# A Fourier filter and a gated two-layer network on one core: the small operations of a normalization moved to GpSimd, chunks of y taken one step later, a third PSUM tile

## The chip, the cores and the metric

The kernel runs on one core of one Trainium2 chip. The metric is the device time of one launch in microseconds, the median of several runs; the times below are for the kernel before the change.

## What is computed

The input x has 4 batches of 3072 tokens with 256 channels. Three blocks follow one another:

```python
X = np.fft.rfft(x, axis=1)                      # filter: along the 3072 tokens
Yr = Xr @ w_r - Xi @ w_i + b_r ; Yi = Xr @ w_i + Xi @ w_r + b_i
Y  = soft_threshold(Yr, 0.01) + 1j * soft_threshold(Yi, 0.01)
y  = np.fft.irfft(Y, n=3072, axis=1)

h = relu(y @ w_in); u, v = h[..., :512], h[..., 512:]
v_n = (v - mean(v)) / sqrt(var(v) + 1e-6)       # per token, over 512 channels
v_s = einsum('ts,bsd->btd', w_spatial, v_n) + b_spatial
x2  = (u * v_s) @ w_out

r = relu(x2 @ w2_in); out = (s * r * r + b) @ w2_out
```

## The kernel before

Three stages follow each other. `attention` does the filter, then the product that gives v, and the normalization of v; `mixing` does the 3072 x 3072 product `w_spatial @ v_n` by a scheme of block sums; `output` does the rest. The change lies in `attention` alone. All products run in two or three passes over a high and a low part of each fp32 operand, so each operand is split: a ScalarE cast gives the high part and a subtraction gives the low one.

The filter is a two-step transform. `s1` is the first step of the forward transform, `g_stage` the second, `mix` the complex product, `g2_stage` the first step of the inverse, and `s3` the last one: 128 calls, 32 for a batch. Between the steps the data goes through DRAM. Four calls of `s3` make one chunk of y (384 tokens), and `v_product` turns a chunk into three tiles of v (128 tokens by 512 channels); three tiles form one normalization group, so there are 32 chunks, 96 products and 32 groups.

The order of the work is written out by hand. Each call issues its matmuls at once and hands its evacuation, as a list of stages, to `Chains`: `ch.step()`, which nearly every call makes once, issues the next stage of every live chain, oldest first; `ch.add` issues the first stage of a new one. `wait` (line 165) is a stage that does nothing. So a chain of n stages is spread over n steps, and every engine then runs its own queue in the order of issue.

For a group, the chain of its third product holds these stages, one per step after the product: `wait`, `stats` (two VectorE operations), `spread` (line 588, variance plus epsilon, 128 x 3), a ScalarE square root (line 612), `rstd` (lines 591 to 596: a reciprocal, two Newton rounds of three operations, one product with the mean; all on VectorE, all 128 x 3, each reading what the one before it wrote), `normal(0)` and `normal(1)`, `normal(2)`, and `store`, three DMAs issued by GpSimd. `normal` runs on ScalarE (line 600) or VectorE (line 602). GpSimd also makes the low parts of x, t and v (line 295).

The chain of the fourth `s3` of a chunk has the stages: ScalarE copy `y_t` of half of the PSUM tile (line 481), VectorE sum `y_sb` (line 463), `store` on the SP queue, `high` (line 472), `low` (line 476), `ready`, which lets `v_product` take the chunk.

The main loop runs over k from 0 to 49 and mixes calls of all stages. After it, `tail[0]` is set and the last loop does what is left of `s3` and `v_product`, about 40 calls of `s3`; each of its turns prefetches one tile for `mixing`, calls `s3_more`, then `v_product` if a chunk is ready, else only `ch.step()`. `s3_more` makes a `v_hi` cast (ScalarE) and a `v_lo` subtraction (GpSimd) in every second turn.

PSUM has four pools in this stage: `pg` (one tile of two banks, used by `g_stage`), `pm`, `pa` and `py` (two tiles of one bank each). The tiles of `s3` come from `py`, so the matmuls of one call wait until the sum `y_sb` of the call two before has read its tile. In the last loop `pg` lies idle.

Of the kernel before, what the change touches and what calls it, by code (L numbers as in the profile page):

```python
# [9 lines left out]
F32 = mybir.dt.float32  # L10
# [5 lines left out]
ALU = mybir.AluOpType  # L16
# [6 lines left out]
N1 = 96  # L23
# [8 lines left out]
EPS = 1e-6  # L32


def f(ap):
    return ap.bitcast(F32)
# [191 lines left out]
def attention(tc, nc, x, w_r, w_i, b_r, b_i, c_f, c_b, c_g, c_v, c_s, zd, vd, yd, vn, chunks, cd, follow, nb=NB):  # L228
# [10 lines left out]
    pg = banks("a_pg", 1, space=PSUM)  # L239
    pm = banks("a_pm", 2, space=PSUM)  # L240
    pa = banks("a_pa", 2, space=PSUM)
    py = banks("a_py", 2, space=PSUM)
    ch = Chains()
# [199 lines left out]
        ch.add([evac])  # L443

    ys = {}

    def s3(j):
        b, n = divmod(j, N2)
        c, o = divmod(n, 4)
        vs.make(j // 2 + 1)  # L450
        hi, lo = vs.t[j // 2]
        ps = py.tile([128, 2, 2, N1], F32, tag="py", name="ps_y")
        for h in range(2):
            for m, t in enumerate((hi, lo)):
                nc.tensor.matmul(ps[:, h].rearrange("p k a -> p (k a)"), t[:, o % 2, h * 128:(h + 1) * 128], cb,
                                 start=m == 0, stop=m == 1)
        if o == 0:
            ys[0] = s3p.tile([128, 2, 4, N1], F32, tag="y_sb", name="y_sb")
        y = ys[0]
        tmp = s3p.tile([128, 2, N1], F32, tag="y_t", name="y_t")  # L460

        def e1():
            nc.vector.tensor_add(y[:, :, o, :], ps[:, :, 0, :], tmp)

        def store():
            (nc.sync if steady[0] else nc.gpsimd).dma_start(
                out=yd[b].rearrange("h p s -> p h s")[:, :, c * 4 * N1:(c + 1) * 4 * N1],
                in_=y.rearrange("p h n a -> p h (n a)"))

        def high():  # L470
            y_hl[8 * b + c] = t = vpool.tile([128, 2, 2, 4 * N1], F32R, tag="y_hl", name="y_hl")
            nc.scalar.copy(t[:, 0], y.rearrange("p h n a -> p h (n a)"))

        def low():
            t = y_hl[8 * b + c]
            nc.vector.tensor_sub(t[:, 1], y.rearrange("p h n a -> p h (n a)"), f(t)[:, 0])

        def ready():
            chunks_ready[0] += 1
        ch.step()  # L480
        ch.add([lambda: nc.scalar.copy(tmp, ps[:, :, 1, :]), e1] + ([store, high, low, ready] if o == 3 else []))

    y_hl = {}
    chunks_ready = [0]
# [1 line left out]
    root = s3c.tile([128, 1], F32, name="root")  # L486
# [73 lines left out]
    def v_product():  # L560

        n = v_done[0]
        v_done[0] += 1
        y = y_hl[n // 3]
        o = (n % 3) * 128
        pool, tag = (pm, "pm") if tail[0] and n % 2 else (pa, "pa")
        ps = pool.tile([128, 512], F32, tag=tag, name="ps_vp")
        c = 0
        for k in range(2):
            for a, w in PASSES:  # L570
                nc.tensor.matmul(ps, y[:, a, k, o:o + 128], win[k][:, w, :], start=c == 0, stop=c == 5)  # L571
                c += 1
        vr = vpool.tile([128, 512], F32, tag="vr", name="vr", bufs=VR)
        bn = vpool.tile([128, 6], F32, tag="bn", name="bn")
        j = n % 3
        if j == 0:
            grp[0] = (vpool.tile([128, 3, 2], F32, tag="mv", name="mv"),
                      vpool.tile([128, 5, 3], F32, tag="rs", name="rs"), [])
        mv, t, vrs = grp[0]
        vrs.append(vr)  # L580
        va, r, z, root, nmr = (t[:, m, :] for m in range(5))

        def stats():
            nc.vector.bn_stats(bn, vr)
            nc.vector.bn_aggr(mv[:, j, :], bn)

        def spread():
            nc.vector.tensor_scalar_add(va, mv[:, :, 1], EPS)

        def rstd():  # L590
            nc.vector.reciprocal(r, root)
            for _ in range(2):
                nc.vector.tensor_mul(z, r, r)
                nc.vector.scalar_tensor_tensor(out=z, in0=z, scalar=-0.5, in1=va, op0=ALU.mult, op1=ALU.mult)
                nc.vector.scalar_tensor_tensor(out=r, in0=z, scalar=1.5, in1=r, op0=ALU.add, op1=ALU.mult)
            nc.vector.scalar_tensor_tensor(out=nmr, in0=mv[:, :, 0], scalar=-1.0, in1=r, op0=ALU.mult, op1=ALU.mult)

        def normal(m):
            if m == 0 or m == 2 and n // 3 % 2 == 0:
                nc.scalar.activation(vrs[m], vrs[m], AF.Identity, bias=nmr[:, m:m + 1], scale=r[:, m:m + 1])  # L600
            else:
                nc.vector.tensor_scalar(vrs[m], vrs[m], r[:, m:m + 1], nmr[:, m:m + 1], op0=ALU.mult, op1=ALU.add)

        def store():
            b, i = divmod(n - 2, 24)
            for m in range(3):
                nc.gpsimd.dma_start(out=vn[b][i + m], in_=vrs[m])
        ch.step()
        nc.scalar.activation(vr, ps, AF.Relu)
        rest = [wait, stats]  # L610
        if j == 2:
            rest += [spread, lambda: nc.scalar.sqrt(root, va), rstd, lambda: (normal(0), normal(1)),
                     lambda: normal(2), store]
        ch.add(rest)

    tail = [False]

    def v_some():
        if v_done[0] < 3 * chunks_ready[0]:
            v_product()  # L620

    for k in range(total + 2):
# [6 lines left out]
        def s3_some(n):  # L629
            nonlocal s3_done  # L630
            for _ in range(n):
                if s3_done < s3_goal:
                    s3(s3_done)
                    s3_done += 1
        if 4 <= k < 16:
            j, h = divmod((k - 4) // 3, 2)
# [34 lines left out]
    def s3_more():  # L671
        nonlocal s3_done
        if s3_done < 32 * nb:
            vs.load(s3_done // 2 + 4)
            s3(s3_done)
            s3_done += 1
            vs.make(s3_done // 2 + 2)
# [3 lines left out]
    while v_done[0] < NV:  # L681
        stage.prefetch()
        s3_more()
        if v_done[0] < 3 * chunks_ready[0]:
            v_product()
        else:
            ch.step()
        if s3_done == 32 * nb:
            ch.step()
        if v_done[0] in (NV - 3, NV - 1):  # L690
            stage.split_first()
# [470 lines left out]
def network(ctx, tc, ins, out):  # L1162
# [25 lines left out]
    with tc.manual_schedule():  # L1188
        attention(tc, nc, ins['x'], ins['w_r'], ins['w_i'], ins['b_r'], ins['b_i'],
                  ins['c_f'], ins['c_b'], ins['c_g'], ins['c_v'], ins['c_s'], zd, vd, yd, vn, chunks, cd,  # L1190
                  lambda: mixing(tc, nc, ins['moe_w_spatial'], vn, md, sd, convert_half)).run()
        output(tc, nc, yd, md, chunks, cd, ins['moe_b_spatial'], ins['moe2_s'], ins['moe2_b'], out)
# [25 lines left out]
```

## Time and profile before the change

| what | value |
|---|---|
| median of 3 runs | 3199.53 us (3198.64 to 3200.73) |
| profiled execution, own time | 3198.13 us |
| its span | 3196.0 us |
| PE busy | 3091.2 us (97%) |
| DVE busy | 2307.5 us (72%) |
| ACT busy | 1427.7 us (45%) |
| POOL busy | 391.2 us (12%) |
| `attention`, to the first matmul burst of `mixing` | about 0 to 568 us |

Times are from the span's start. PE is TensorE, DVE is VectorE, ACT is ScalarE, POOL is GpSimd. Busy shares are means over three stages with different limits; the change can be judged only inside the first 570 us.

### The profile page before, as it was taken

What the parts mean: (1) busy time and instruction counts of PE and PEld (TensorE: products, weight loads), DVE (VectorE), ACT (ScalarE), POOL (GpSimd) and SP (SyncE); (2) the same over time, 40 slices, a digit from 0 to 9 for tenths busy, and PEclk for the clock granted to TensorE, in tenths of its full rate; (3) what the DMA queues carried; (4) which work ended last, traced back from release to release, by engine and by line L of the source; (5) the groups of instructions that cost most, each with busy time, mean ns of one, the idle gap of its engine ahead of it and who ended that gap; (6) DMA issues with size and microseconds to landing.
All of it is one profiled execution on the core that took longest, in us unless ns stands there. A gap on an engine that the chain in (4) does not pass through costs nothing.

```text
span 3196.0 us, 46503 instructions
## 1 busy us (share of the span) xinstructions
PE 3091.2 (97%) x17960; PEld 3016.2 (94%) x17960; DVE 2307.5 (72%) x3495; ACT 1427.7 (45%) x2243; POOL 391.2 (12%) x497
## 2 busy tenths in 40 slices
PE   7989998999999999999999999999999999999999
PEld 4988986999999999999999989999999999999999
DVE  5877988887878888888878755656566656656564
ACT  4776766433334333433434334444444444444443
POOL 2665544022000210000000100000000000000000
PEclk9999999999999999999999999999999999999999
DMA  7987759487456956466471621111111111110210
GB/s 233 288 264 236 232 173 332 158 310 298 159 198 195 356 216 230 147 214 257 152 244 38 238 90 54 48 50 65 55 65 55 65 55 65 55 62 30 71 45 15
DMA packets 230517, 488.30 MB, mean 153 GB/s; under 512 B 22356, under 2 KB 116376, under 8 KB 230296
## 3 DMA queue, kind: packets, MB, share of 16 engines
q1 hardware_dynamic: 197112, 353.44, 33.4%
q0 software_dynamic: 33184, 131.90, 11.2%
q8 instruction: 140, 2.29, 0.3%
q14 instruction: 81, 0.66, 0.1%
HBM read 322.72 MB, written 162.53 MB: 152 GB/s over the span
## 4 chain that ended last, share of the span: by engine, by line
PE 76%; DVE 13%; DMA 5%; ACT 3%; issue 2%; POOL 0%; SPq 0%; ACTq 0%; DVEq 0%; POOLq 0%
PE acc L849 27%; PE ps_h L1059 17%; PE oacc L1080 17%; PE ps_o L1040 4%; PE ps_u L1022 4%; PE ps_m L407 3%; PE ps_vp L571 2%; DMA st_a<-in_moe_w_spatial_dram 1%; DVE kept L866 1%; DVE a_hl L830 1%; DVE b_hl L830 1%; DMA st_b<-t 1%; PE ps_z L333 1%; DMA st_b<-vn 1%; PE ps_g L360 1%
## 5 line engine op out<-in xcount | busy, mean ns | idle before, releaser
L849 PE MATMUL acc<-a_hl,b_hl 128*128 128x384 f32 x7056 | 1240.7, 337 | 30.4 <-DVE kept L866 11.5
L849 PEld LDWEIGHTS acc<-a_hl,b_hl 128*128 128x128 f32 x7056 | 1234.3, 189 | 36.8 <-ACT kept L870 11.9
L1059 PE MATMUL ps_h<-x_hl,w 128*128 128x384 f32 x3072 | 580.8, 337 | 1.5 <-ACT x_hl L1043 0.9
L1080 PE MATMUL oacc<-q_hl,w 128*128 128x384 f32 x3072 | 575.5, 337 | 0.5 <-DVE q_hl L1066 0.5
L1059 PEld LDWEIGHTS ps_h<-x_hl,w 128*128 128x128 f32 x3072 | 543.4, 188 | 2.1 <-ACT x_hl L1043 1.3
L1080 PEld LDWEIGHTS oacc<-q_hl,w 128*128 128x128 f32 x3072 | 537.1, 188 | 0.9 <-DVE q_hl L1066 0.8
L826 ACT CAST a_hl<-a 128x768 fp32r<-128x768 f32 x253 | 211.7, 837 | 522.6 <-PE acc L849 440.8
L1066 DVE TENSOR_TENSOR q_hl<-r,q_hl 128x768 fp32r<-128x768 f32 x256 | 245.4, 959 | 230.7 <-ACT q_hl L1065 230.7
L1064 DVE TENSOR_TENSOR r<-r 128x768 f32<-128x768 f32 x256 | 244.8, 956 | 204.6 <-ACT r L1063 204.6
L1065 ACT CAST q_hl<-r 128x768 fp32r<-128x768 f32 x256 | 213.6, 835 | 301.7 <-DVE r L1064 301.7
L1063 ACT ACTIVATE r<-ps_h 128x768 f32<-128x768 f32 x256 | 208.2, 813 | 310.9 <-PE ps_h L1059 307.4
L830 DVE TENSOR_TENSOR a_hl<-a,a_hl 128x768 fp32r<-128x768 f32 x253 | 241.2, 953 | 138.4 <-ACT a_hl L826 137.8
L830 DVE TENSOR_TENSOR b_hl<-b,b_hl 128x512 fp32r<-128x512 f32 x295 | 201.8, 684 | 0.0
L826 ACT CAST b_hl<-b 128x512 fp32r<-128x512 f32 x295 | 181.8, 616 | 0.0
L571 PE MATMUL ps_vp<-win,y_hl 128*128 128x512 f32 x576 | 155.7, 407 | 17.8 <-ACT v_sb L438 14.7
L867 POOL DMA_DIRECT2D md<-kept x112 | 60.5, 540 | 828.9 <-DVE kept L866 824.5
L1022 PE MATMUL ps_u<-y_hl,w 128*128 128x384 f32 x768 | 145.7, 340 | 1.8 <-DVE y_hl L1008 1.8
L1040 PE MATMUL ps_o<-g,w 128*128 128x384 f32 x768 | 139.3, 337 | 1.6 <-DVE g L1030 1.0
L571 PEld LDWEIGHTS ps_vp<-win,y_hl 128*128 128x128 f32 x576 | 103.2, 193 | 39.8 <-ACT v_sb L438 16.3
L1022 PEld LDWEIGHTS ps_u<-y_hl,w 128*128 128x128 f32 x768 | 135.5, 190 | 3.1 <-DVE y_hl L1008 2.1
L1040 PEld LDWEIGHTS ps_o<-g,w 128*128 128x128 f32 x768 | 133.5, 188 | 2.5 <-DVE g L1030 1.6
L866 DVE TENSOR_TENSOR kept<-acc,kept 128x768 f32<-128x768 f32 x112 | 102.8, 950 | 22.0 <-PE acc L849 21.0
(138 smaller groups left out, 3702.5 us busy)
## 6 DMA issues: line engine op xcount, KB each, us to landing
a<-in_moe_w_spatial_dram SPq DMA_DIRECT2D x144, 384.0 KB, 4.8
b<-vn SPq DMA_DIRECT2D x168, 256.0 KB, 4.9
md<-kept POOLq DMA_DIRECT2D x112, 384.0 KB, 5.2
m<-md SPq DMA_DIRECT2D x56, 768.0 KB, 6.4
st_a<-in_moe_w_spatial_dram SPq DMA_DIRECT2D x72, 384.0 KB, 5.4
vn<-vr POOLq DMA_DIRECT2D x96, 256.0 KB, 4.0
s<-a POOLq DMA_DIRECT2D x48, 384.0 KB, 5.8
x_f<-in_x_dram SPq DMA_DIRECT2D x32, 384.0 KB, 6.1
```

The lines of the kernel that those rows point to most:

```text
L571: nc.tensor.matmul(ps, y[:, a, k, o:o + 128], win[k][:, w, :], start=c == 0, stop=c == 5)
L826: nc.scalar.copy(s[:, 0, :], t)
L830: sub(s[:, 1, :], term.pop((kind, n)), f(s)[:, 0, :])
L849: nc.tensor.matmul(acc[d][:, h, 0:TH], b[:, m, d * 128:(d + 1) * 128], a[:, w, h * TH:(h + 1) * TH], start=fresh and i == 0 and c == 0, st ...
L1022: nc.tensor.matmul(ps[:, d, 0:TH], win[k][:, a, o:o + 128], y[:, w, k, :], start=c == 0, stop=c == 5)
L1040: nc.tensor.matmul(ps[:, h, 0:TH], wo[k // 2][:, a, o:o + 128], g[:, w, k, :], start=c == 0, stop=c == 11)
L1059: nc.tensor.matmul(ps[:, e, 0:TH], w[:, a, o:o + 128], x[:, i, j, :], start=c == 0, stop=c == 5)
L1063: nc.scalar.activation(r, ps[:, :, 0:TH], AF.Relu)
L1064: nc.vector.tensor_mul(r, r, r)
L1065: nc.scalar.copy(s[:, 0], r)
L1066: nc.vector.tensor_sub(s[:, 1], r, f(s)[:, 0])
L1080: nc.tensor.matmul(ps[:, h, 0:TH], w[:, a, o:o + 128], s[:, i, e, :], start=ff == 0 and c == 0, stop=ff == 2 * NP - 1 and c == 2)
```

## The change

- `spread` runs on GpSimd.
- In `rstd` only the reciprocal stays on VectorE. The seven VectorE operations behind it become ten GpSimd operations: each Newton round has four in place of three, and the product with the mean has two in place of one. All are 128 x 3 and each reads what the one before it wrote.
- A `wait` stage stands between `rstd` and the normals, which are issued one step later, and so are the three stores of a group.
- A `wait` stage stands between `low` and `ready` of a chunk.
- In the last loop every third call of `s3` takes its PSUM tile from `pg`.

```diff
     def s3(j):
-        ps = py.tile([128, 2, 2, N1], F32, tag="py", name="ps_y")
+        if tail[0] and j % 3 == 0:
+            ps = pg.tile([128, 4, 256], F32, tag="pg", name="ps_y")[:, 0:2, 0:2 * N1].rearrange(
+                "p h (k a) -> p h k a", k=2)
+        else:
+            ps = py.tile([128, 2, 2, N1], F32, tag="py", name="ps_y")
...
-        ch.add([lambda: nc.scalar.copy(tmp, ps[:, :, 1, :]), e1] + ([store, high, low, ready] if o == 3 else []))
+        ch.add([lambda: nc.scalar.copy(tmp, ps[:, :, 1, :]), e1] + ([store, high, low, wait, ready] if o == 3 else []))
...
         def spread():
-            nc.vector.tensor_scalar_add(va, mv[:, :, 1], EPS)
+            nc.gpsimd.tensor_scalar_add(va, mv[:, :, 1], EPS)
 
         def rstd():
             nc.vector.reciprocal(r, root)
+            g = nc.gpsimd
             for _ in range(2):
-                nc.vector.tensor_mul(z, r, r)
-                nc.vector.scalar_tensor_tensor(out=z, in0=z, scalar=-0.5, in1=va, op0=ALU.mult, op1=ALU.mult)
-                nc.vector.scalar_tensor_tensor(out=r, in0=z, scalar=1.5, in1=r, op0=ALU.add, op1=ALU.mult)
-            nc.vector.scalar_tensor_tensor(out=nmr, in0=mv[:, :, 0], scalar=-1.0, in1=r, op0=ALU.mult, op1=ALU.mult)
+                g.tensor_mul(z, r, r)
+                g.tensor_mul(z, z, va)
+                g.tensor_scalar(z, z, -0.5, 1.5, op0=ALU.mult, op1=ALU.add)
+                g.tensor_mul(r, z, r)
+            g.tensor_mul(nmr, mv[:, :, 0], r)
+            g.tensor_scalar_mul(nmr, nmr, -1.0)
...
-            rest += [spread, lambda: nc.scalar.sqrt(root, va), rstd, lambda: (normal(0), normal(1)),
+            rest += [spread, lambda: nc.scalar.sqrt(root, va), rstd, wait, lambda: (normal(0), normal(1)),
                      lambda: normal(2), store]
```

## Rows read from the trace of the kernel before

**Rows 1.** Busy time by stretch: main loop, last loop, its end; us and instruction counts.

```profile
core 0: us, PE busy (x) PEld busy (x) DVE busy (x) ACT busy (x) POOL busy (x), PEclk, DMA share, GB/s
182.00:470.00 288.00, 271.08 (x1854) 248.79 (x1852) 246.61 (x572) 197.53 (x432) 146.02 (x147) 0.98 0.67 219
476.00:556.00 80.00, 65.22 (x340) 50.18 (x338) 70.67 (x212) 53.52 (x122) 38.71 (x47) 1.00 0.94 329
556.00:576.00 20.00, 13.34 (x56) 11.76 (x56) 16.54 (x43) 11.77 (x20) 4.14 (x8) 0.83 0.35 128
```

**Rows 2.** Groups on DVE, 182 to 470 us: busy us, mean ns | idle before, releaser.

```profile
L594 DVE SCALAR_TENSOR_TENSOR rs<-rs 128x3 f32<-128x3 f32 x40 | 18.3, 459 | 1.4
L593 DVE TENSOR_TENSOR rs<-rs 128x3 f32<-128x3 f32 x40 | 11.0, 276 | 1.4
L595 DVE SCALAR_TENSOR_TENSOR rs<-rs 128x3 f32<-128x3 f32 x40 | 8.6, 214 | 1.4
L588 DVE TENSOR_SCALAR rs<-mv 128x3 f32<-128x3 f32 x20 | 7.6, 382 | 0.7 <-issue 0.2
L596 DVE SCALAR_TENSOR_TENSOR rs<-mv,rs 128x3 f32<-128x3 f32 x20 | 5.4, 269 | 0.7
```

**Rows 3.** Two groups on PE: the first of 182 to 470, the second of 476 to 556.

```profile
L571 PE MATMUL ps_vp<-win,y_hl 128*128 128x512 f32 x348 | 94.7, 408 | 13.6 <-ACT v_sb L438 11.9 <-ACT vr L609 0.8 <-DVE y_hl L476 0.8
...
L455 PE MATMUL ps_y<-cb,v_hi 96*128 96x192 f32 x78 | 21.1, 296 | 14.8 <-DVE y_sb L463 14.7
```

**Rows 4.** Timeline at 318 us: start, duration, engine, line, operation [idle before].

```profile
318.63 2.40 POOL L295 TENSOR_TENSOR t_l<-t_f,t_h 128x1024 fp32r<-128x1024 f32 x1 [5.23 <-ACT t_h L291]
318.67 2.38 DVE L594 SCALAR_TENSOR_TENSOR rs<-rs 128x3 f32<-128x3 f32 x1
```

**Rows 5.** Timeline at 465 to 471 us, one group of the main loop.

```profile
464.93 2.53 POOL L295 TENSOR_TENSOR v_lo<-v_f,v_hi 96x512 fp32r<-96x512 f32 x2 [4.47 <-ACT v_hi L291]
...
466.20 1.29 DVE L593 TENSOR_TENSOR rs<-rs 128x3 f32<-128x3 f32 x1
...
467.52 0.17 DVE L594 SCALAR_TENSOR_TENSOR rs<-rs 128x3 f32<-128x3 f32 x1
...
468.71 0.81 ACT L600 ACTIVATE vr<-vr,rs 128x512 f32<-128x512 f32 x1 [2.52 <-DVE rs L596]
...
470.56 2.03 PE L571 MATMUL ps_vp<-win,y_hl 128*128 128x512 f32 x4 [2.21 <-ACT v_sb L438]
```

**Rows 6.** The two groups on ACT that wait for the small operations, 476 to 556.

```profile
L600 ACT ACTIVATE vr<-vr,rs 128x512 f32<-128x512 f32 x15 | 12.2, 816 | 9.2 <-DVE rs L596 9.2
...
L612 ACT ACTIVATE rs<-rs 128x3 f32<-128x3 f32 x10 | 2.0, 204 | 16.7 <-DVE rs L588 16.7
```

**Rows 7.** Timeline of one group in the last loop, 494 to 499 us.

```profile
494.28 0.62 ACT L291 CAST v_hi<-v_f 96x512 fp32r<-96x512 f32 x1
...
495.29 1.29 POOL L295 TENSOR_TENSOR v_lo<-v_f,v_hi 96x512 fp32r<-96x512 f32 x1
...
495.62 1.01 DVE L588 TENSOR_SCALAR rs<-mv 128x3 f32<-128x3 f32 x1
...
496.66 0.20 ACT L612 ACTIVATE rs<-rs 128x3 f32<-128x3 f32 x1 [1.75 <-DVE rs L588]
...
496.77 0.30 ACT L481 COPY y_t<-ps_y 128x192 f32<-128x192 f32 x1
...
498.49 0.81 ACT L600 ACTIVATE vr<-vr,rs 128x512 f32<-128x512 f32 x1 [0.93 <-DVE rs L596]
```

**Rows 8.** Chain that ended last, in order of time: start, us, what; eight chunks apart.

```profile
485.33 0.86 DVE y_hl L476
...
550.46 0.87 DVE y_hl L476
```

**Rows 9.** Timeline of POOL at the span's start: a write without a read.

```profile
0.28 0.10 POOL L1199 MEMSET const-float32-1.0<- 128x1 f32 x1
```

**Rows 10.** Busy time by stretch, in `mixing`, columns as in the first group.

```profile
730.00:740.00 10.00, 10.00 (x59) 10.00 (x58) 5.28 (x8) 3.24 (x6) 2.16 (x4) 1.00 1.03 417
```

More of the change, by code (lines that the diff above doesn't have):

```diff
@@ L445, in attention @@
     ys = {}
+    tail = [False]
     def s3(j):
@@ L611, in v_product @@
         if j == 2:
-            rest += [spread, lambda: nc.scalar.sqrt(root, va), rstd, lambda: (normal(0), normal(1)),
+            rest += [spread, lambda: nc.scalar.sqrt(root, va), rstd, wait, lambda: (normal(0), normal(1)),
                      lambda: normal(2), store]
         ch.add(rest)
-    tail = [False]
     def v_some():
```

## Prediction, made before the changed kernel ran

> **What bounds the kernel now.** I read the busy time by stretch first, then the groups of instructions in two stretches, then timelines of single groups of the normalization, and last the chain that ended last. All of the change lies before 570 us, and there in two places with different limits.
>
> In the main loop, 182 to 470 us, PE is busy 271.1 of 288 us [rows 1]; at most 17 us are to be had there. DVE is at 246.6, ACT at 197.5, POOL at 146.0. The operations that the change takes off DVE make 18.3 + 11.0 + 8.6 + 7.6 + 5.4 = 50.9 us of its 246.6 [rows 2], for 20 groups. Yet PE hardly waits for DVE: 11.9 of its idle time is a product that waits for ScalarE's copy `v_sb` to free a PSUM tile, and 0.8 for a low part of y [rows 3]. Rows 5 show where such a wait comes from: GpSimd makes two low parts from 464.93 to 467.46; the small operation at 466.20, 0.17 us at its neighbour, takes 1.29 and ends when GpSimd does; ScalarE stands 2.52 us before the normal at 468.71; `v_sb` comes late and PE loses 2.21. Rows 4 show the same with a larger GpSimd subtraction: 2.38 beside 2.40. So in the main loop the cost is a stall of ScalarE, in order, behind the small operations.
>
> In the last loop, 476 to 556 us, no engine is full: PE 65.2 of 80, DVE 70.7, ACT 53.5, POOL 38.7 [rows 1]. Eight chunks take 550.46 - 485.33 = 65.1 us, so 8.14 us for each [rows 8]. ScalarE explains them: 53.5 us busy and 16.7 + 9.2 = 25.9 us of standing before the square root and the normals [rows 1, 6], 79.4 of 80. Per group that is 1.67 before the square root and 0.92 before the normals. A circle of dependences therefore sets the pace: normals, ScalarE's own queue, statistics, `spread`, square root, Newton rounds, next normals. PE's 14.7 us of waiting for `y_sb` [rows 3] follow from it.
>
> **The change part by part.** *Price of a small GpSimd operation.* No row shows one with inputs. A `v_lo` of 512 elements takes 1.29, a `t_l` of 1024 takes 2.40 [rows 7, 4]: 2.17 ns an element, and 2 x 1.29 - 2.40 = 0.18 us for none. To the next that depends on it there is a gap: on DVE 467.52 - 467.49 = 0.03 [rows 5]. With 0.03 to 0.10 I get 0.21 to 0.28 and take 0.25. Bounds: 0.10, the write without a read [rows 9]; 0.36, if the passage from one to the next costs as much as the operation. So 11 operations are 2.75 us of GpSimd per group (1.1 to 4.0).
>
> *`spread` and `rstd` in the last loop.* A chunk has eight steps, and the chunk's order of issue is: step 1 `v_hi` and `v_lo`, step 2 `spread`, step 3 the square root, step 4 `rstd`, step 5 (now 6) the normals, step 5 another `v_hi` and `v_lo`, and the stores at the end. Before, DVE's `spread` ran at 495.62 while GpSimd had the `v_lo` of 495.29, and took 1.01; it ended 0.05 after it [rows 7]. After, `spread` stands in GpSimd's queue right behind that same `v_lo`. It waits for it as before and then takes 0.25: from the end of the cast to the square root 1.29 + 0.25 + about 0.1 for gaps = 1.65, against 1.67 now. Nothing is won there. Before the normals, ten operations of 0.25 replace seven that start 0.20 apart (467.52 less 467.49 plus 0.17): 2.5 against 1.4, so +1.1. The added step lets ScalarE do a copy and a cast of 0.30 and 0.62 [rows 7] first; they overlap their neighbours by some 0.1 each, so -0.7. The stall becomes 0.92 + 0.4 = 1.3. Both together: 2.95 for 2.59, +0.36 per chunk, and with ten groups in the stretch **+4 us**. At 0.36 per operation it is 1.75 + 2.4 = 4.15, +15 us. At 0.10 it is 1.5 + 0 = 1.5, -11 us, but the DMA engines stop it earlier: they move 329 GB/s at a share of 0.94 here, 350 at a full share [rows 1], so the stretch's 26.3 MB need 75.2 us, -5. (With the 417 of [rows 10] it would be 63; that stretch only loads, so I keep -5.) Behind the waiting square root and normals on ScalarE stand `y_t`, `v_hi`, `y_hl` and the Relu that frees the product's PSUM tile; s3 and the products on PE wait for these. Behind a waiting operation on GpSimd stand `v_lo` and the stores of vn. `v_lo` is made two pairs ahead, more than three turns before its matmuls, so a delay of 2.75 us is hidden by some 6 us; without that lead it would be paid in each chunk.
>
> *The same in the main loop.* The groups come 14.4 us apart (288 / 20), so no circle sets the pace, only single stalls count. DVE is relieved of 50.9 / 20 = 2.5 us per group. The chain takes 2.5 in place of 1.4 plus what GpSimd's port took (43.3 - 140 x 0.17 = 19.5 us for 20 groups, 1.0), which now comes back as GpSimd's own queue; so +1.1, against a step of 0.7 to 1.0 that lies between. The stall of the normals stays about what it was. But what ScalarE does in that step is in part the evacuation that PE waited for: in rows 5 `v_sb` can come before the normal, not after. I give back a third of the 11.9 us: **-4**. Bounds: -12 (all of it) and +6, if `spread` behind a subtraction of 1.29 holds the square root by 0.3 more in each of 20 groups.
>
> *The stores of vn* come a step later: one microsecond of a buffer of nine tiles, three chunks long. Nothing. No DMA moves on the SP queue.
>
> *Chunks of y a step later.* In the last loop two steps make a turn and the chunk is looked for in the second one: `ready` moves from the fifth step to the sixth, both before the same look. Nothing. In the main loop a product can move by one slot; it can save the 0.8 us of [rows 3] and cost as much: 0, +-1.
>
> *The third PSUM tile.* It lets `s3` wait for the sum of three calls before and can remove the 14.7 us of [rows 3]. The pace is set elsewhere, so they become slack: 0. Were PE the limit, it would be worth up to 1.5 us per chunk; that is in the lower end of the range. `pg` is free by then.
>
> *The end of the stage*, 556 to 576: one group's `spread` no longer waits for splits on DVE, its chain is 1.1 longer: 0, +-1.
>
> **Sum.** +4 - 4 + 0 = 0 against the profiled 3198.13, whose median of runs is 1.4 higher: 3199.5, so **3200**.
>
> **A rule against the change.** Rows 4 and 5 show a DVE operation that ends with the GpSimd operation beside it. The Trainium skill, "SBUF — State Buffer", section "SBUF: two separate sides", says that the two share a port pair which the first holds alone for a whole instruction; by that rule, with which these rows agree, the stall does not vanish but passes to DVE's next operation with two inputs, such as `low`. The Trainium skill, "Perfetto Trace Analysis", section "Optimizing Scalar/DVE Operations", says that moving work between these two may not help for this reason. This is the third rival below.
>
> **The rivals.**
> 1. *Relief* (0.29). Small operations cost 0.10 to 0.15, and ScalarE's stalls shrink. For it: DVE's 50.9 + 20 us of work gone, PE free in the last loop by the third tile. Against it: 0.18 by the two subtractions, and the DMA share of 0.94. It gives -5 in the last loop and -8 in the main one: **3186**.
> 2. *GpSimd's queue becomes the limit* (0.26). Place: `spread` behind `v_lo`, and the chain of ten, both in ScalarE's way. From 0.30 per operation on it decides: there the last loop has 1.7 + 1.8 = 3.5 for 2.59, +9, and the main loop's -4 falls to about +2: **3211**. For it: the circle above has no slack. Against it: the step that hides 0.7.
> 3. *The stalls change their owner* (0.10). DVE's other operations wait for GpSimd instead, PE sees nothing in the main loop: 0, and +4 in the last: **3203.5**.
>
> **How the numbers follow.** The forecast, 3200, has 0.35. A measurement here tells about 0.2%, 6.4 us, from no change. Forecast and rival 3 lie within it (0.45); faster 0.29, slower 0.26. The forecast's own range is 3193 to 3207. To leave out no more than 2 in 10 it reaches to rival 1 and rival 2 with the bounds of the price: 3184 to 3214.
>
> **What would show it.** Small GpSimd operations start 0.21 to 0.28 apart; ScalarE's stalls in the last loop near 1.65 and 1.3 per group; chunks there 8.4 to 8.6 us apart; PE's waits for `y_sb` there near zero; in the main loop DVE near 196 us busy and PE's waits for `v_sb` near 8 us. It is wrong if the small operations lie outside 0.15 to 0.30, if the DMA engines carry far over 350 GB/s in the last loop, or if the time is won or lost behind 576 us.

## The result, and the profile after

The changed kernel takes **3227.05 us**, the median of 6 runs (3223.10 to 3231.71), beside 3200.34 us for the kernel before on the same chips (6 runs, 3198.64 to 3203.80). The ratio is 1.008 [1.007, 1.009]: 26.7 us slower. The prediction said 3200 and its range ended at 3214. The profiled execution took 3229.8 us, its span is 3226.5.

The loss lies ahead of the product of `mixing`, in two places. The last matmul of the main loop's inverse stage (`g2_stage`, L433) starts at 474.7 us before and at 489.6 after: +15. The last product of v ends at 561.9 before and at 588.5 after, so the last loop takes 98.9 us in place of 87.2: +11.7. Busy time by stretch, each kernel with its own ends of the two loops (columns as in [rows 1]). Before:

```profile
182.00:475.00 293.00, 275.52 (x1873) 252.65 (x1871) 249.60 (x579) 199.68 (x437) 147.66 (x149) 0.98 0.67 218
475.00:562.00 87.00, 70.77 (x364) 54.39 (x363) 75.97 (x224) 58.41 (x131) 39.64 (x48) 1.00 0.90 316
```

After:

```profile
182.00:490.00 308.00, 281.34 (x1869) 256.63 (x1868) 210.90 (x416) 199.57 (x435) 194.97 (x368) 0.96 0.64 205
490.00:589.00 99.00, 83.41 (x365) 66.04 (x365) 69.58 (x149) 59.81 (x132) 63.82 (x164) 0.84 0.86 284
```

The work did move: DVE 249.6 to 210.9 in the main loop, POOL 147.7 to 195.0. Yet TensorE needs longer for the same number of matmuls. In the main loop 9.2 of the 15 us are more idle time (26.7 for 17.5) and 5.8 are longer matmuls: the granted clock is 0.96 for 0.98. In the last loop its idle time is the same (15.6 for 16.2), and the matmuls take 12.6 us more at a granted clock of 0.84 for 1.00.

The waits say where the relief went. Main loop, ACT and then DVE of after (engine, line, what it waited for: us in total, times, longest):

```profile
ACT vr L608 <- POOL rs L604: 46.3, 20, 4.0
...
ACT yh L420 <- DVE mt L419: 15.2, 20, 2.2
ACT rs L620 <- POOL rs L593: 12.1, 13, 2.1
...
DVE vr L610 <- POOL rs L604: 52.4, 20, 5.1
```

The same of before, ACT:

```profile
ACT vr L600 <- DVE rs L596: 41.0, 20, 4.0
...
ACT yh L420 <- DVE mt L419: 3.6, 7, 0.9
ACT rs L612 <- DVE rs L588: 3.4, 4, 1.3
```

The change took 50.9 us of small operations off VectorE [rows 2], and VectorE now stands for 52.4 us before its own normal (L610) until GpSimd has finished them; before, this wait did not exist, since VectorE had made the numbers itself. ScalarE stands 25.6 us more in three places: 5.3 before the normals, 8.7 before the square root, 11.6 before `yh`, which waits for VectorE. Its waits for TensorE's products of v are 10.4 us shorter (17.5 for 27.9).

One group of the last loop, beside [rows 7] (start, duration, engine, line, operation, idle before):

```profile
521.79 1.28 POOL L295 TENSOR_TENSOR v_lo<-v_f,v_hi 96x512 fp32r<-96x512 f32 x1 [1.40 <-ACT v_hi L291]
...
523.16 0.23 POOL L593 TENSOR_SCALAR rs<-mv 128x3 f32<-128x3 f32 x1
...
523.42 0.20 ACT L620 ACTIVATE rs<-rs 128x3 f32<-128x3 f32 x1 [1.71 <-POOL rs L593]
...
523.66 0.18 DVE L596 RECIPROCAL rs<-rs 128x3 f32<-128x3 f32 x1 [1.11 <-ACT rs L620]
...
523.92 0.20 POOL L599 TENSOR_TENSOR rs<-rs 128x3 f32<-128x3 f32 x1 [0.53 <-DVE rs L596]
...
524.20 0.19 POOL L600 TENSOR_TENSOR rs<-rs 128x3 f32<-128x3 f32 x1
...
526.43 0.23 POOL L604 TENSOR_SCALAR rs<-rs 128x3 f32<-128x3 f32 x1
...
526.64 1.26 POOL L295 TENSOR_TENSOR v_lo<-v_f,v_hi 96x512 fp32r<-96x512 f32 x1
526.70 0.81 ACT L608 ACTIVATE vr<-vr,rs 128x512 f32<-128x512 f32 x1 [1.64 <-POOL rs L604]
526.70 1.48 DVE L610 TENSOR_SCALAR vr<-vr,rs 128x512 f32<-128x512 f32 x1 [1.41 <-POOL rs L604]
```

The small operations start 0.28 us apart (523.92 to 524.20; ten from 523.92 to 526.66). From the end of the reciprocal to the normals it is 526.70 - 523.84 = 2.86 us; before, from 496.89 + 0.19 = 497.08 (the reciprocal on the chain shown at the end of this section) to the normal at 498.49 in [rows 7], it was 1.41. Then `v_lo`, next in GpSimd's queue, starts together with VectorE's normal, which takes 1.48 where it took 0.54 before. VectorE's fifteen normals of the last loop take 16.6 us in place of 8.0.

The chain that ended last shows the pace of the last loop (start, us, what). After, two chunks between each of these, so 9.09 us for a chunk; before it was 8.14 [rows 8]:

```profile
537.81 0.74 ACT y_hl L477
...
555.98 0.74 ACT y_hl L477
...
574.16 0.74 ACT y_hl L477
```

Before, that chain ran almost wholly on one engine. Between 490 and 507 us all its pieces but one stretch on ScalarE (499.21 to 501.26) are VectorE's, one behind the other, with the small operations among them:

```profile
496.62 0.26 DVE y_sb L463
...
496.89 0.19 DVE rs L591
...
498.29 0.04 DVE rs L596
...
498.37 0.35 DVE y_sb L463
498.72 0.47 DVE vr L602
```

### The profile page after: what moved, and what is told of

Same layout as the page of the kernel before. It is cut to its first block, busy times and chain, and to the rows that moved or that the text cites. A ratio compares the mean times of both kernels' runs of the same rounds, so it can differ in the third digit from the quotient of the medians.

```text
span 3226.5 us, 46568 instructions
## 1 busy us (share of the span) xinstructions
PE 3109.7 (96%) x17960; PEld 3030.8 (94%) x17960; DVE 2257.9 (70%) x3239; ACT 1429.3 (44%) x2243; POOL 466.6 (14%) x849
## 4 chain that ended last, share of the span: by engine, by line
PE 74%; DVE 10%; DMA 6%; POOL 4%; issue 4%; ACT 3%; SPq 0%; ACTq 0%; POOLq 0%; DVEq 0%
PE acc L856 27%; PE ps_h L1066 16%; PE oacc L1087 16%; PE ps_o L1047 4%; PE ps_u L1029 4%; PE ps_vp L576 2%; PE ps_m L407 2%; DMA st_a<-in_moe_w_spatial_dram 1%; DVE kept L873 1%; DVE a_hl L837 1%; POOL v_lo L295 1%; DVE b_hl L837 1%; DMA st_b<-t 1%; PE ps_z L333 1%; DMA st_b<-vn 1%
## 5 line engine op out<-in xcount | busy, mean ns | idle before, releaser
L856 PEld LDWEIGHTS acc<-a_hl,b_hl 128*128 128x128 f32 x7056 | 1232.5, 189 | 38.4 <-ACT kept L877 13.5
L576 PE MATMUL ps_vp<-win,y_hl 128*128 128x512 f32 x576 | 170.3, 433 | 23.8 <-ACT v_sb L438 15.8
L576 PEld LDWEIGHTS ps_vp<-win,y_hl 128*128 128x128 f32 x576 | 110.1, 206 | 51.8 <-ACT v_sb L438 17.3
```

The costliest lines, as they stand in the source:

```text
L856: nc.tensor.matmul(acc[d][:, h, 0:TH], b[:, m, d * 128:(d + 1) * 128], a[:, w, h * TH:(h + 1) * TH], start=fresh and i == 0 and c == 0, st ...
```

## The experiments

Four parts of the change can be taken apart. P: the small operations on GpSimd (`spread` and the chain behind the reciprocal). W: the wait before the normals. C: the wait of a chunk. T: the third PSUM tile. Each row gives the median, the ratio to the kernel before on the same chip with its 95% interval, and two places in the one profiled execution of that run: the start of the last `g2_stage` matmul, where the main loop ends, and of the last product of v, where the last loop ends. Executions of one kernel differ by some microseconds (3223 to 3232 us in after), so differences of these places are no surer than that. e11, e12, e14 and e15 have C in both loops.

| run | what it is | us | ratio | g2 | last product |
|---|---|---|---|---|---|
| before | | 3200 | | 474.7 | 561.9 |
| after | P W C T | 3227.05 | 1.0080 [1.0070, 1.0090] | 489.6 | 588.5 |
| e1 | W C T | 3206.89 | 1.0024 [1.0014, 1.0034] | 480.8 | 566.8 |
| e2 | P | 3253.68 | 1.0169 [1.0153, 1.0184] | 512.5 | 616.2 |
| e3 | after, `spread` on VectorE | 3218.44 | 1.0058 [1.0043, 1.0073] | 482.4 | 576.6 |
| e4 | after, chain on VectorE | 3209.51 | 1.0031 [1.0020, 1.0042] | 483.0 | 568.8 |
| e5 | C | 3198.57 | 0.9994 [0.9985, 1.0004] | 472.6 | 559.8 |
| e6 | T | 3202.70 | 1.0005 [0.9996, 1.0015] | 474.1 | 563.0 |
| e7 | W | 3205.87 | 1.0016 [1.0006, 1.0025] | 480.7 | 566.4 |
| e8 | after, three waits | 3203.33 | 1.0009 [0.9999, 1.0018] | 461.9 | 565.4 |
| e9 | after, one Newton round | 3189.02 | 0.9969 [0.9956, 0.9982] | 463.4 | 551.3 |
| e10 | after, low parts of v on VectorE | 3243.35 | 1.0138 [1.0123, 1.0153] | 509.5 | 604.1 |
| e11 | C; P and three waits in the main loop, before in the last | 3188.66 | 0.9961 [0.9947, 0.9975] | 461.8 | 551.2 |
| e12 | C; three waits in the main loop alone, no P | 3208.77 | 1.0027 [1.0016, 1.0038] | 479.9 | 567.2 |
| e13 | before, one Newton round | 3184.28 | 0.9951 [0.9936, 0.9966] | 465.9 | 549.3 |
| e14 | C; P W in the main loop alone | 3212.47 | 1.0040 [1.0025, 1.0055] | 486.0 | 573.9 |
| e15 | C; P W T in the last loop alone | 3211.68 | 1.0034 [1.0020, 1.0048] | 476.4 | 573.4 |
| e16 | after, normals on ScalarE | 3257.09 | 1.0179 [1.0162, 1.0196] | 508.6 | 615.3 |
| e17 | after, normals on VectorE | 3225.90 | 1.0076 [1.0061, 1.0091] | 485.2 | 587.8 |

### The parts by themselves

**e1**, the change without its move, all small operations on VectorE as in before:

```diff
-            nc.gpsimd.tensor_scalar_add(va, mv[:, :, 1], EPS)
+            nc.vector.tensor_scalar_add(va, mv[:, :, 1], EPS)
...          rstd as in the kernel before
```

> The changed kernel with every small operation back on VectorE; the three waits and the third PSUM tile stay. Theory A (ScalarE and VectorE stand in order behind the ten GpSimd operations and behind the spread): all of the loss goes, 3195 to 3202 us. Rival B (the added waits and the PSUM tile reorder the work and cost the time): it stays at 3220 or more. Half of it each: near 3212.

Measured: 7.5 us slower than before, between the theories. The move itself is then some 20 us of the loss (3227.05 - 3206.89 = 20.2), the rest comes from the steps that were put in.

**e2**, the move alone, without W, C and T:

```diff
-            rest += [spread, ..., rstd, wait, lambda: (normal(0), normal(1)),
+            rest += [spread, ..., rstd, lambda: (normal(0), normal(1)),
```

> The move to GpSimd alone: no wait before the normals, none before the chunk is ready, no third PSUM tile. Theory A: at least the whole loss, and more by the step that no longer lies between, 0.7 us for each of 32 groups at most: 3225 to 3250 us. Rival B: near the kernel before, 3200.

Measured: 54 us slower than before, just above theory A's range and twice the loss of the whole change. ScalarE and VectorE both stand for 96 us before the normals, in 32 groups, so 3 us in each:

```profile
ACT vr L608 <- POOL rs L604: 96.9, 32, 5.2
DVE vr L610 <- POOL rs L604: 96.3, 32, 5.1
```

So with the chain on GpSimd the added wait is worth some 27 us, 0.8 us for each group, if C and T do as little there as they do in the kernel before (e5 and e6).

**e3** and **e4** put back `spread`, or the chain:

```diff
# e3
-            nc.gpsimd.tensor_scalar_add(va, mv[:, :, 1], EPS)
+            nc.vector.tensor_scalar_add(va, mv[:, :, 1], EPS)
# e4: rstd as in the kernel before, spread stays on GpSimd
```

> The changed kernel with the spread alone back on VectorE. Theory A splits the loss by what ScalarE stood longer in the traces: before the square root 33.6 for 23.5 us, before the normals 67.2 for 54.1, so the spread has some 10 of 23 us: 3213 to 3220 us. If the chain on GpSimd carries all of it: 3225. If the place of the spread in GpSimd's queue carries all: 3200.

> The changed kernel with the reciprocal's followers back on VectorE; only the spread is on GpSimd. Theory A: 3205 to 3212 us. If the chain on GpSimd carries all of the loss: 3200. If the spread carries all: 3225.

Both came as theory A had them. Measured against e1: the chain alone costs 11.5 us, `spread` alone 2.6, both 20.2. The chain is the larger part. That they cost 6 us more together than one by one is not clear of the intervals, which are 3 to 5 us wide on each side for each of these runs.

The two places in the table tell the parts apart by loop. The main loop ends at 474.7 in before, at 480.8 with the added steps (e1), at 482.4 with the chain on GpSimd too (e3), at 489.6 with `spread` as well (after): 6.1, 1.6 and 7.2 us. The last loop takes 87.2, 86.0, 94.2 and 98.9 us: nothing for the steps, 8.2 for the chain, 4.7 for `spread`. With the chain alone on GpSimd, VectorE's normal already waits nearly as long as in after (all 32 groups, 70.1 in after):

```profile
DVE vr L610 <- POOL rs L604: 67.2, 32, 5.1
```

In the main loop it is 49.4 us, and yet that loop ends only 1.6 us later than with the chain on VectorE: there the work taken off VectorE and its new standing about cancel.

**e5**, **e6** and **e7** add one step each to the kernel before:

```diff
# e5
+  [store, high, low, wait, ready]
# e6
+        if tail[0] and j % 3 == 0:
+            ps = pg.tile(...)
# e7
+            rest += [spread, ..., rstd, wait, lambda: (normal(0), normal(1)),
```

> The kernel before with the wait ahead of a chunk's release alone. The run with all small operations on VectorE was 7.5 us slower than before, 6 of them in the main loop. Theory C (later chunks let products slip, and PE has nothing in their place): 3203 to 3208 us. Rival (the late normals do it): 3199.

> The kernel before with the third PSUM tile in the last loop alone. PE's 14.7 us of waiting for the sum there become slack, the pace is set by ScalarE's standing: 3197 to 3200 us. If PE was the limit: 3185 to 3192.

> The kernel before with the wait between the reciprocal's step and the normals alone. Theory A: ScalarE stands some 35 us less before the normals, and the time falls: 3188 to 3197 us. Rival of theory C: the normals hold other evacuations up one step later, 3203 to 3208.

Measured: C and T, each alone in the kernel before, change nothing that can be measured, as the prediction had it. Without the move W does not win the time of theory A but costs 5.4 us, as the rival had it (0.16% [0.06, 0.25]). The waits on ACT in e7's main loop show why: the normals wait less (10.0 for 41.0), and the same time stands one instruction further on, before `yh`:

```profile
ACT yh L420 <- DVE mt L419: 44.0, 23, 4.6
...
ACT vr L605 <- DVE rs L601: 10.0, 6, 3.3
```

VectorE is late as a whole here (252.6 busy of 299 us), so a later place in the order only changes which of ScalarE's instructions meets it.

### How long the chain is

**e9** shortens the chain on GpSimd from ten dependent operations to six; the second Newton round is left out:

```diff
-            for _ in range(2):
+            for _ in range(1):
                 g.tensor_mul(z, r, r)
```

> The changed kernel with one Newton round in place of two, which leaves out a part of the square root's refinement: six dependent GpSimd operations in place of ten, 1.1 us less per group. Theory A: of the standing before the normals (67.2 us on ScalarE, 2.1 per group) some 1.0 goes in each of 32 groups, and with it 8 to 20 us: 3207 to 3219 us. If the length of the chain does not matter: 3227.

Measured: 38.0 us faster than after, far beyond theory A's 8 to 20. Four operations of 0.28 us in 32 groups are 35.8 us: within the noise, the whole length that was taken out came off the time. The main loop ends 26.2 us earlier, the last loop is 11.0 shorter (87.9 for 98.9). The run also leaves less work in GpSimd's queue; e8 below, with all of that work, tells the two apart for the main loop, and no run does for the last. The waits before the normals, up to 680 us, are halved (70.1 and 67.2 in after):

```profile
DVE vr L610 <- POOL rs L604: 36.5, 28, 4.0
ACT vr L608 <- POOL rs L604: 33.6, 29, 2.8
```

**e13** does the same to the kernel before, on VectorE:

```diff
-            for _ in range(2):
+            for _ in range(1):
                 nc.vector.tensor_mul(z, r, r)
```

> The kernel before with one Newton round in place of two, so seven dependent VectorE operations fewer by three per group; the second refinement is left out. In the main loop of before the three take 0.28 + 0.46 + 0.21 = 0.95 us per group with what GpSimd's port adds. Theory S (the whole length of the chain is paid in each of the 32 groups, whichever engine it runs on): 3200 - 30, so 3168 to 3176, and the wait of the first normal for the statistics falls from 54 to some 30 us. Rival H (on VectorE the chain was hidden in the main loop, it is GpSimd's queue that makes it visible; only the last loop, where 0.2 x 3 are on the circle, pays): 3200 - 10 x 0.6, 3192 to 3196.

Measured: 14.7 us faster than before, between the two theories. Theory S had counted too much as removed: three of seven operations go, but the ones that stay take over the delays beside GpSimd. These are the groups of e13 from 182 to 600 us; in before L593 takes 15.0, L594 22.3, L595 12.5 (64 of each) and L596 7.3 us:

```profile
L594 DVE SCALAR_TENSOR_TENSOR rs<-rs 128x3 f32<-128x3 f32 x32 | 13.8, 431 | 1.1
L593 DVE TENSOR_TENSOR rs<-rs 128x3 f32<-128x3 f32 x32 | 13.0, 405 | 1.1
L595 DVE SCALAR_TENSOR_TENSOR rs<-rs 128x3 f32<-128x3 f32 x32 | 6.3, 196 | 1.1
...
L596 DVE SCALAR_TENSOR_TENSOR rs<-mv,rs 128x3 f32<-128x3 f32 x32 | 5.2, 163 | 1.1
```

So 57.1 us became 38.3: 18.8 us, and with 3 x 32 gaps of 0.03 some 22. Two thirds of that came off the time, 8.8 us of it in the main loop and 3.8 in the last. The chain's length was on the path before the change as well, less strictly than after it.

**e8** keeps the long chain and moves the normals two steps further away from it, **e10** takes the low parts of v out of GpSimd's queue:

```diff
# e8
-            ... rstd, wait, lambda: (normal(0), normal(1)),
+            ... rstd, wait, wait, wait, lambda: (normal(0), normal(1)),
# e10: the stream of v
-  3, 4, "dve", "pool")
+  3, 4, "dve", "dve")
```

> The changed kernel with three waits before the normals in place of one. Theory A: the normals are issued two steps (some 1.8 us) later, so the standing before them, 2.1 us per group, nearly goes and the time comes down by 10 to 15: 3211 to 3217 us. If the load of GpSimd's queue or the port costs the time, and not the standing: 3222 to 3230.

> The changed kernel with the low part of v made by VectorE (0.69 us each in place of 1.29 on GpSimd). Theory Q (the small operations are late because they queue behind these subtractions on GpSimd): spread and chain start up to 1.3 us earlier in each group, and the time falls to 3205 to 3217 us although VectorE gets 44 us of work. If only the chain's own length matters: 3225 to 3235.

e8, measured: 24 us faster than after, more than either theory had, and no different from before. GpSimd's work is that of after, so in the main loop, where all of the gain lies, the load of its queue is not what costs the time. The result is two loops of opposite sign, with the columns of [rows 1]:

```profile
400.00:460.00 60.00, 60.00 (x425) 55.72 (x424) 48.38 (x97) 42.41 (x93) 37.50 (x73) 1.00 0.56 187
460.00:500.00 40.00, 32.51 (x158) 25.48 (x157) 23.85 (x53) 21.01 (x47) 23.95 (x62) 0.91 0.90 299
500.00:540.00 40.00, 33.01 (x141) 25.44 (x139) 24.55 (x56) 22.50 (x53) 25.97 (x66) 0.83 0.87 297
```

The main loop ends 13 us earlier than in before, TensorE full to the end; the last loop takes 103.5 us for 87.2, and for 98.9 in after. The two more steps do take away most of the standing before the normals there (VectorE's falls from 12.8 to 3.3 us, ScalarE's from 14.3 to 8.9), and the loop is longer all the same: the standing is not its price by itself. That it lacks other work for the time of the chain, which the main loop has, fits this but is not shown by itself. Nor does every added step lengthen it: with no wait at all (e2) it takes 103.7.

e10, measured: 16 us slower than after, above both theories. The main loop ends 20 us later still (509.5). Freeing GpSimd's queue of `v_lo` does not help where VectorE must take the work; how much of the delay of `spread` behind `v_lo` alone costs is not told by it.

### Which loop, and which engine stands

**e14** and **e15** make the change in one of the loops alone:

```diff
+        in_tail = tail[0]
# e14: GpSimd and one wait in the main loop; VectorE, no wait, no third tile in the last
+        rstd = rstd_vector if in_tail else rstd_pool
# e15: the other way round, with the third tile
+        rstd = rstd_pool if in_tail else rstd_vector
```

> The changed kernel, whose main loop stays as it is (GpSimd, one wait), with the small operations back on VectorE, no wait and no third PSUM tile in the last loop. Theory S (the loss is two sums that add, +15 us until the main loop's last g2 and +11.7 us in the last loop): 3227 - 11.7 = 3213 to 3218. Rival L (the last loop is long because it starts late and at a lower TensorE clock, not for GpSimd's operations in it): 3223 to 3228, and the granted clock stays near 0.87 between 500 and 580 us.

> The counterpart: the main loop of before (VectorE, no wait) with the change's last loop (GpSimd, one wait, third PSUM tile, chunks a step later). Theory S: 3200 + 11.7 = 3209 to 3214, the main loop's last g2 matmul near 475 us as in before. Rival L (what the last loop lost comes from its late start): 3198 to 3204. The prediction's +4 for this loop would be 3204.

Measured: +13.5 and +12.7 us, and 26.2 together are the 26.7 of the whole change. Theory S holds (e15 lies in its range, e14 half a microsecond under it) and L falls: e15, whose main loop is that of before and ends within 2 us of it, has a last loop of 97.0 us; e14, which comes to it 11 us later than before does, has one of 87.9. Last loop of e14:

```profile
486.00:574.00 88.00, 72.39 (x367) 56.00 (x366) 76.52 (x227) 58.73 (x131) 40.26 (x49) 0.98 0.92 321
```

And of e15:

```profile
476.00:573.40 97.40, 81.06 (x368) 64.46 (x367) 67.33 (x144) 59.70 (x132) 63.05 (x159) 0.88 0.86 282
```

The low clock is not that of the late start. It goes with GpSimd's operations in this loop, also without the third tile (e2 had 0.87 there); the third tile alone gave 0.92 (e6). A somewhat lower clock does not lengthen the loop by itself: e1 ran it at 0.94 in 86 us, with 75.7 us of matmuls. No run has a clock of 0.84 to 0.89 without the operations on GpSimd.

**e16** and **e17** give all normals to ScalarE, or to VectorE:

```diff
-            if m == 0 or m == 2 and n // 3 % 2 == 0:
+            if True:        # e16; e17: if False:
```

> The changed kernel with all three normals of a group on ScalarE (0.81 us each), so that VectorE never waits for GpSimd's last small operation; ScalarE still does and has 1.5 x 0.81 x 32 = 39 us more of work. Theory A (ScalarE's standing in order, with the copies that free PSUM behind it, is what TensorE pays): 3235 to 3265, TensorE's waits for v_sb above 16 us. Theory D (VectorE's new standing of 52 us in the main loop, with the sums y_sb behind it, is what costs): 3205 to 3218, and the waits for y_sb fall.

> The counterpart: all three normals on VectorE, so that ScalarE never waits for GpSimd's last small operation (46 us of its standing in the main loop go, with 39 us of its work); VectorE still waits and has the normals more. Theory A: 3203 to 3214, TensorE's waits for v_sb near zero. Theory D: 3228 to 3245, TensorE's waits for y_sb above 14 us.

Measured: 3257.1, as theory A had it, and 3225.9, between the two theories. D falls with e16: the wait of VectorE is gone and the kernel is 30 us slower than after. A falls with e17: ScalarE no longer waits for GpSimd's chain, and nothing is won. The waits on ACT in e17's main loop show that VectorE's standing is handed on to ScalarE through its next products:

```profile
ACT xl L377 <- DVE xl L374: 42.0, 18, 4.7
ACT yh L420 <- DVE mt L419: 34.1, 21, 5.7
```

In after these two were 6.3 and 15.2 us. So the loss cannot be put down to one engine's standing: each runs its queue in order, and the other needs its results. What either standing costs by itself these two runs do not tell, since each also gave 39 us of normals more to the engine that still waits.

### A version that is faster than both

**e11** puts P with three waits in the main loop and leaves the last loop as it was before (with C, without T); **e12** is the same without P:

```diff
+            rest += [spread, ..., rstd] + [wait] * (0 if in_tail else 3)
+        rstd = rstd_vector if in_tail else rstd_pool       # e11; e12: always VectorE
```

> Main loop with the small operations on GpSimd and three waits before the normals, last loop with them on VectorE and no wait, as before; chunk late, no third PSUM tile. The run with three waits ended its main loop 13 us earlier than the kernel before and lost 16 in the last loop. If these two add up independently: 3184 to 3190 us. If the gain of the main loop is only work put off into the last loop: 3198 to 3204.

> The same with the small operations on VectorE in the main loop too: three waits there, none in the last loop. If the later normals bring the gain of the main loop: 3184 to 3192 us, as on GpSimd. If it needs VectorE relieved of 50 us: 3196 to 3206.

Measured: e11 takes 3188.66 us (3185.73 to 3189.95), 0.9961 [0.9947, 0.9975] of before: 11.7 us faster than before and 38 faster than after. e12 is 8 us slower than before, a little above its second theory. So the waits alone lose, the move alone loses (e2), and together, with the last loop left as it was, they win. The main loop of e11; ACT's waits before its normals there are 21.8 us:

```profile
182.00:462.00 280.00, 271.96 (x1877) 249.64 (x1877) 218.61 (x414) 200.12 (x434) 198.74 (x365) 0.99 0.69 227
```

And TensorE's wait for `v_sb` in it, 14.1 us in before:

```profile
PE ps_vp L576 <- ACT v_sb L438: 2.7, 4, 0.9
```

## Why the prediction was wrong

**The price of a small GpSimd operation was right.** 0.28 us measured, 0.21 to 0.28 forecast. Point by point against what it said would show: the stalls of ScalarE in the last loop are 1.79 and 1.43 us a group (19.7 in 11 and 14.3 in 10) for 1.65 and 1.3; DVE in 182 to 470 us is busy 197.8 for "near 196"; the loss lies ahead of `mixing`. Wrong are the pace of the chunks (9.09 for 8.4 to 8.6), the waits for `y_sb` in the last loop (8.9 for "near zero") and the waits for `v_sb` in the main loop (15.6 for 8). None of its three signs of being wrong came: the price lies inside 0.15 to 0.30, the DMA engines carry 284 GB/s in the last loop, and the time is lost ahead of `mixing`.

**The step that failed in the main loop:** "only single stalls count", and the -4 us that was taken from it. The one stall that the prediction followed, ScalarE's before the normals, came out as it had it, "about what it was" (46.3 us for 41.0), and the chain's move by itself ends this loop only 1.6 us later (e1 to e3). Three other terms failed. The -4 was to come from TensorE's waits for `v_sb`, which did not fall (15.6 us for 14.1). The added step was counted only as cover for the longer chain; it does cover it (27 us, e2 to after), but by itself it ends the loop 6 us later (e1, e7), and the sum had nothing for that. `spread` in GpSimd's queue had a bound of +6 and nothing in the forecast; it ends the loop 7.2 us later (e3 to after), and in after ScalarE stands 8.7 us more before the square root than in before. The last two and the chain's 1.6 are the 15 us. What the prediction overlooked stands in the waits: it listed what is queued behind ScalarE's normal, but not VectorE's normal, which reads the same GpSimd result. So VectorE's 50.9 us of relief came back as 52.4 us of standing and paid for none of this. That the chain's length counts in this loop too is shown by e9 and e13 (26.2 and 8.8 us), and that the change in this loop alone costs 13.5 us by e14.

**The step that failed in the last loop:** "ScalarE explains them". Its standing there was the effect. The chain of before runs from one VectorE operation to the next (busy 76.0 of 87 us), and ScalarE's 27.5 us of waits ended whenever VectorE came round. The forecast of those waits was close (2.95 for each of ten groups, 34.0 us measured), yet their 6.5 us more are only about half of the loss. For +4 it became +11.7: 8.2 by the chain, and 4.7 by `spread`, which the prediction had at nothing. What it left out lies on VectorE: 12.8 us of waiting before its normal and 9.8 before the reciprocal, neither there before, and normals that take 8.6 us more beside `v_lo`. How these add up to the 0.95 us by which a round is longer is read from single groups and not measured by a run of its own. A round now goes from VectorE to GpSimd and back twice where it had stayed in one queue but for the square root. That the operations on GpSimd are the cause, and not the late start, is shown by e14 and e15; e9 shows that it is their number and length, but not whether by the chain or by what queues behind it on GpSimd. How much of the 11.7 us the lower clock adds, through products that a round waits for, stays open.

**The rivals.** Rival 2, GpSimd's queue as the limit, named the right places, `spread` behind `v_lo` and the chain of ten. It was to decide from 0.30 us an operation and decided at 0.28, and its 3211 is 16 us short. But in the main loop it is not the queue's load that limits: e8 has the same load there and ends that loop 28 us earlier than after. Rival 1 is refuted by the price. Rival 3, stalls that change their owner, named VectorE as the new owner and then held that TensorE would see nothing in the main loop; e17 shows one way in which it can, by `xl` and `yh` on ScalarE.

**The zeros held.** C and T measure 0.9994 and 1.0005, each alone in the kernel before. Behind the last product the profiled execution loses another 4 us in `output`; the stretch from its first product to the end takes 1363 to 1368 us in the profiled kernels, e6 and e12 among the long ones, so this is not the change's.

**The rule against the change** had its effect, in another place than `low`. At 526.70 VectorE's normal takes 1.48 us beside a `v_lo` of 1.26 that began 0.06 earlier, and ends 0.28 after it; over the main loop the normals take 0.77 us on average for 0.54 before. The Trainium skill, "SBUF — State Buffer", section "SBUF: two separate sides", has the port pair that the two engines share held by one of them for a whole instruction. The row at 526.70 agrees with that. The small operations that `v_lo` used to hold up were taken away, and the next VectorE instruction, the normal, met it in their place.

## What to carry to other kernels

Moving a chain of dependent small operations to an idle engine need not pay for the busy time that it frees, if the engine it leaves has to wait for the chain's result: look for every reader of the result, on every in-order queue, and set the chain's whole length against the work that stands between. How many steps to put between differs from loop to loop (three steps and GpSimd in the main loop, none and VectorE in the last, gained 12 us where one step in both lost 27). Where a loop runs on a single engine's queue nearly from end to end, a part that takes longer on another engine (here 2.86 us for 1.41) lengthens each round, idle as that engine may be.

## What the runs showed of the hardware

A 128 x 3 operation on GpSimd takes 0.195 to 0.23 us, and one that reads the result of the one before it starts 0.28 us after it; on VectorE it is 0.17 and 0.20 (without a GpSimd operation beside it). The hand-over from VectorE's reciprocal to GpSimd took 0.08 us (523.84 to 523.92), from GpSimd to ScalarE or VectorE 0.03 to 0.04 (523.39 to 523.42, 526.66 to 526.70). TensorE's granted clock followed the loop: with the same matmuls in a longer round it was 0.84 in the last loop of after and 0.88 in that of e15, for 1.00 in before and 0.98 in e14 (1.00 is the 2.4 GHz level). But in e6, where only the third PSUM tile was added, the clock was 0.92 and the last loop took 88.9 us for 87.2; of 7.1 us of longer matmuls, 5.4 fell into idle time. What lowers it is not told by these runs.
